# Moving the preparation of the next pair of heads: its uses of the scratch banks spread over six double steps

## The chip, the cores and the metric

The kernel runs on one core of one Trainium2 chip. The metric is device time in microseconds (us) for one execution, the median over runs. The engines that matter here are the tensor engine (PE, whose weight loads have a row of their own, PEld), the vector engine (DVE), the scalar engine (ACT), GpSimd (POOL) and SyncE (SP), whose queue issues nearly all DMAs. Each engine works through its own list of instructions in the order in which the program gives them, and they wait for one another by semaphores.

## The reference, cut to what matters

```python
# q, k, v: (4, 8, 768, 64) float32 ; centroids: (8, 16, 64)
q_assign = argmax(q_n @ c_n.T, -1); k_assign = argmax(k_n @ c_n.T, -1)   # 16 clusters a head
mask   = q_assign[:, :, :, None] == k_assign[:, :, None, :]
scores = where(mask, q @ k.T / sqrt(64), -1e9)
x = (softmax(scores) @ v)                  # -> (3072, 512), heads side by side
h = x @ w_in                               # (512, 2048), float64 in memory
out = (h * clip(h + 3, 0, 6) / 6) @ w_out  # (2048, 512), float64 in memory
```

It is attention in which a query sees only the keys of its own cluster, followed by a feed-forward block (FFN) with a hard-swish gate. Both weight matrices arrive as 64-bit floats and are turned into 32-bit floats on the chip.

## The kernel before, in words

**Tiling.** The 32 heads (4 batches of 8) are worked on as 16 pairs; the two heads of a pair lie side by side on the partitions. A pair takes 12 steps: two halves of 384 queries by six chunks of 128 keys. The main loop (L647) takes two steps at a time, a *double step*, so that a pair has six of them. They are called r0, r2, r4, r6, r8 and r10 here, after the variable `r`, and they are counted by k = 0 to 95 over the kernel: double step k belongs to pair k // 6.

**What a double step holds**, in the order in which it is issued to the engines:

- `scores` twice (L375). On PE: transposed scores of a key chunk against 384 queries for both heads (`ps`, L370), first from the float32 transposes `xf`, then from `xm`, the one-hot cluster codes, which push the scores of a key of another cluster far down. On ACT: `exp` of them into `ex` (L382). On POOL: the running sum `acc` of `ex` (L386, L389).
- `attn_v` twice (L393), for the two steps before: `pv` on PE (L399). At the end of a half, in r0 and r6, ACT copies the sum into `num` (L405).
- In r2 and r8 `divide` (L411) for the half that has ended: PE sums `acc` over the partitions into `pd` (L420), DVE takes the reciprocal `rcp` (L424) and multiplies it with `num` (L425) into `xT`, the input of the FFN. The check `in_range` (two operations of ACT, L432 and L433) is put on a list and issued at the end of the following double step.
- The preparation of the *next* pair, by `prep_items` (L588): four `turn`s (L287), each three transposes on PE into `pqk` (L294) and an ACT copy to `xf` (L296); `cluster_scores` (L303), matmuls into `pcs` (L307) and an ACT copy to `cs`; `route` (L314), three transposes into `pr` (L318) and then on DVE the maximum `mx` (L321) and two comparisons that write `one_hot` (L327), first the part of the queries and then that of the keys; and three `route_turn`s (L343), each four small matmuls into `po` (L350) and an ACT copy to `xm` (L354). `route` also puts `count` (ACT, `seen`, L336, twice) on the list of checks.
- Items of the FFN (`fill`), taken in turns with the items of the preparation: first an item of the FFN, then one of the preparation, and so on. Their matmuls go into `ph`, `py`, `X` and `Y`; ACT and DVE take them out.
- Steps of decoding the weights, a list of 160 (32 chunks of five: `split`, `join`, `power`, `rest`, `total`, L203). All five have an operation on DVE, of about 0.7 us; `split` and `power` have one on ACT too (L214, L230). `split` also issues the DMA of the next chunk. How many are taken in a double step stands in `share` (L613).
- The checks from the list of the double step before.

In r6 the loads of q and k of the pair after next and of v of the next pair are issued on SP (L666).

**Banks.** `scratch` (L167) gives out the PSUM banks for short-lived results: `pqk`, `pcs`, `pr`, `po` and `pd`. Up to k = 47 these are the two banks of the pool `psum_m`, which the FFN's `ph` shares from k = 27 on; from k = 48 it is the single bank of `psum_t`, which up to then serves the decoding (`wtop`). A pair uses scratch eleven times: four `pqk`, one `pcs`, one `pr`, three `po`, two `pd`. A bank can be used again once the engine that empties it is done.

**Stages.** For k = 0 to 26 there is no FFN work. For k = 27 to 47 sixteen items `up` of the FFN's first batch are spread, at most one to a double step. For k = 48 to 51 there are ten FFN items to a double step, from k = 52 one or two, and after k = 95 the rest of the FFN.

The order is written out by hand (`manual_schedule`): each engine has its instructions in the order in which the code issues them.

Of the kernel before, what the change touches and what calls it, by code (L numbers as in the profile page):

```python
# [24 lines left out]
NPAIR = NG // 2  # L25
# [91 lines left out]
def fast_path(ctx, tc, ok, q, k, v, centroids, moe_w_in, moe_w_out, out):  # L117
# [49 lines left out]
    def scratch(shape, name):  # L167

        if st["early"]:
            return psum_m.tile(shape, F32, name=name, tag="m")  # L170
        return psum_t.tile(shape, F32, name=name, tag="t")
# [26 lines left out]
    def load_weights(i):  # L198
        if i < len(chunks):
            st["raw", i] = rawp.tile([P, WC, 2], U32, name="raw")  # L200
            nc.sync.dma_start(st["raw", i], chunks[i][1])
# [85 lines left out]
    def turn(g, part):  # L287
        if part == 0:
            st["xf", g] = xp.tile([P, NC2, P], F32, name="xf")
        qk, xf = st["qk", g], st["xf", g]  # L290
        pt = scratch([P, NHC, P], "pqk")
        for i in range(NHC):
            j = part * NHC + i
            nc.tensor.transpose(out=pt[:, i], in_=qk[:, j // NCH, j % NCH], identity=ident)  # L294
        dst = xf[:, part * NHC : (part + 1) * NHC]
        nc.scalar.copy(out=dst, in_=pt)  # L296
        if part == 3:
            st.pop(("qk", g))
# [4 lines left out]
    def cluster_scores(g):  # L303
        c0, xf = (2 * g) % H * C, st["xf", g]
        ps = scratch([P, 512], "pcs")[:, 0 : NC2 // 4 * P]
        for a in range(4):
            nc.tensor.matmul(  # L307
                ps[a * 2 * C : (a + 1) * 2 * C], lhsT=cnT[:, c0 : c0 + 2 * C], rhs=xf[:, a::4],
                start=True, stop=True,
            )  # L310
        cs = st["cs", g] = rtp.tile([P, NC2 // 4, P], F32, name="cs")
        nc.scalar.copy(out=cs, in_=ps)

    def route(g):  # L314
        cs = st.pop(("cs", g))
        pr = scratch([P, NC2, 2, C], "pr")
        for i in range(NC2 // 4):
            nc.tensor.transpose(out=pr[:, 4 * i : 4 * i + 4], in_=cs[:, i], identity=ident)  # L318
        pr = pr.rearrange("p j t c -> p (j t) c")
        mx = rtp.tile([P, 2 * NC2], F32, name="mx")  # L320
        nc.vector.reduce_max(out=mx, in_=pr, axis=AX.X)  # L321
        oh = one_hot.rearrange("p j (t c) -> p j t c", t=2)[:, :, :, 0:C]
        pr = pr.rearrange("p (j t) c -> p j t c", t=2)
        mx = mx.rearrange("p (j t) -> p j t", t=2)
        halves = [slice(0, NCH), slice(NCH, NC2)]
        for sl, op in zip(halves, (ALU.is_ge, ALU.is_lt)):
            nc.vector.tensor_tensor(  # L327
                out=oh[:, sl], in0=pr[:, sl],
                in1=mx[:, sl].unsqueeze(3).to_broadcast([P, NCH, 2, C]), op=op,
            )  # L330


        def count():
            for a, sl in enumerate(halves):
                seen = rtp.tile([P, NCH, 2, C], BF16, name="seen")
                nc.scalar.activation(  # L336
                    out=seen, in_=oh[:, sl], func=ACT.Copy, scale=1.0 - 2 * a,
                    accum_out=counts[:, a, g : g + 1],
                )

        later.append(count)

    def route_turn(g, part):  # L343
        if part == 0:
            st["xm", g] = xp.tile([P, NC2, P], BF16, name="xm")
        xm = st["xm", g]
        po = scratch([P, 4, P], "po")
        for i in range(4):
            j = part * 4 + i
            nc.tensor.matmul(  # L350
                po[:, i], lhsT=one_hot[:, j], rhs=(ident_q if j < NCH else ident_k),
                start=True, stop=True,
            )
        nc.scalar.copy(out=xm[:, part * 4 : part * 4 + 4], in_=po)  # L354
# [232 lines left out]

    def prep_items(g, r):  # L588

        if g >= NPAIR:  # L590
            return []
        if r in (0, 2):
            return [lambda: turn(g, r), lambda: turn(g, r + 1)]
        return {
            4: [lambda: cluster_scores(g)],
            6: [lambda: route(g)],
            8: [lambda: route_turn(g, 0), lambda: route_turn(g, 1)],
            10: [lambda: route_turn(g, 2)],
        }.get(r, [])

    per_pair = 2 * NCH
    per_batch = NKT * per_pair
    total = NPAIR * per_pair
# [6 lines left out]


    decode = [step for i in range(NW) for step in decoding_steps(i)]
    share = {0: 5, 2: 3, 4: 4, 6: 1, 8: 3, 10: 4}  # L613
    READY, DECODED = per_batch + lag_d, 2 * per_batch

    END = 2 * per_batch + NCH + 2
# [13 lines left out]
    with tc.manual_schedule():  # L630
        nc.scalar.dma_start(cen, centroids.rearrange("h c d -> (h c) d"))
        load(0, "q", "k")
        constants()
        load(0, "v")
        load_weights(0)
        centroid_norm()
        for part in range(4):
            turn(0, part)
        load(1, "q", "k")
        scores_qk(0)  # L640
        scores_qk(1)
        cluster_scores(0)
        route(0)
        for part in range(3):
            route_turn(0, part)

        for n in range(0, total + lag_d + 2, 2):  # L647
            g, r = divmod(n, per_pair)
            for i in (n, n + 1):
                if i < total:  # L650
                    scores(i)
            for i in (n - lag_v, n - lag_v + 1):
                if 0 <= i < total:
                    attn_v(i)
            m = n - lag_d + 1
            if m >= 0 and m % NCH == NCH - 1:
                later.append(divide(m))
            prep = prep_items(g + 1, r)
            if r == 4 and prep:
                prep.pop()()  # L660
            if n == DECODED:
                st["early"] = False
            if m >= 0 and m % per_batch == per_batch - 1:
                fill += (fast_items if m >= per_batch else ffn_items)(m // per_batch)
            if r == 6:
                load(g + 2, "q", "k")  # L666
                load(g + 1, "v")
            want = items_by(n + 2) - done if n < total else len(fill)
            want = min(want, len(fill))
            done += want  # L670
            for i in range(max(len(prep), want)):
                if i < want:
                    fill.pop(0)()
                if i < len(prep):
                    prep[i]()
            for step in decode[: share[r]]:
                step()
            del decode[: share[r]]
            if n >= DECODED and (n - DECODED) // 2 < 8:
                weight_sums((n - DECODED) // 2)  # L680
            for check in checks:
                check()
            checks, later[:] = later[:], []

        for check in checks:
            check()
# [384 lines left out]
```

## Time and profile before

| | |
|---|---|
| median of 3 runs | 1073.45 us (1073.01 to 1074.95) |
| the profiled execution | 1073.12 us, its span 1071.3 us, granted clock of the tensor engine 0.999 |
| PE busy | 1039.3 us (97% of the span), weight loads 670.0 us |
| DVE, ACT, POOL busy | 394.1, 391.2, 294.1 us |
| k = 0 to 26, 27 to 47, 48 to 95 and the rest | about 0 to 133, 133 to 271, 271 to 1071 us |

The profiler's rows give the start of an instruction and its duration. A matmul's end is modelled and covers some of the start of the next, so the time that a matmul really takes up on PE is best read from one start to the next. In an answer of the timeline a row is: start in us, duration in us, engine, line, operation, tiles written and read, form, number of instructions merged, and in brackets the idle time of the engine ahead of it with what ended it.

### The profile page before, as it was taken

Reading aid. Unit: us, or ns where it says so; the run is one execution under the profiler, and the core shown is the slowest. Engines: PE = TensorE matmul, PEld = TensorE weight load, DVE = VectorE, ACT = ScalarE, POOL = GpSimd, SP = SyncE. Lnnn points to the kernel's source line nnn. Section 1 sums busy time; section 2 is a strip of 40 time slices with the busy share of each in tenths; the row PEclk is TensorE's granted clock in tenths of the full one; section 3 lists DMA queues with packets and bytes.
Section 4 is the critical chain, followed back from the end, with each engine's and each line's share of the span. In section 5 each row is a group of like instructions: output and inputs, shape, how many; then the busy total and the mean of one; then the engine's idle time right before and its main releaser. Section 6 shows DMA issues by size and latency. Waiting matters only on the chain.

```text
span 1071.3 us, 12819 instructions
## 1 busy us (share of the span) xinstructions
PE 1039.3 (97%) x5218; PEld 670.0 (63%) x5218; DVE 394.1 (37%) x609; ACT 391.2 (37%) x798; POOL 294.1 (27%) x171
## 2 busy tenths in 40 slices
PE   6999999999999999999999999999999999999997
PEld 3444444444445545676767676667677678888886
DVE  5788865565122103420331331332231232314141
ACT  6888865655212202423332432332423230201010
POOL 3777644444011002223223222323232320000000
PEclk9999999999999999999999999999999999999999
DMA  6444443143001000010202002020100000000000
GB/s 158 100 123 128 129 103 94 59 104 64 10 27 38 1 20 11 22 24 20 45 1 56 10 1 59 6 45 1 35 1 1 20 1 20 1 20 1 20 1 24
DMA packets 83540, 42.89 MB, mean 40 GB/s; under 512 B 76304, under 2 KB 76304, under 8 KB 83472
## 3 DMA queue, kind: packets, MB, share of 16 engines
q1 hardware_dynamic: 83328, 41.95, 15.2%
q8 instruction: 43, 0.70, 0.3%
q14 instruction: 25, 0.20, 0.1%
q10 hardware_dynamic: 144, 0.03, 0.0%
HBM read 35.68 MB, written 6.29 MB: 39 GB/s over the span
## 4 chain that ended last, share of the span: by engine, by line
PE 97%; ACT 2%; DVE 1%; issue 0%; POOL 0%; POOLq 0%; DVEq 0%
PE ph L520 24%; PE ps L370 16%; PE pv L399 13%; PE Y L538 12%; PE X L538 9%; PE ph L456 8%; PE py L473 8%; PE pqk L294 2%; PE pd L420 2%; PE pcs L307 1%; PE po L350 1%; ACT g_sb L443 1%; ACT xm L354 1%; PE pr L318 1%; ACT xf L296 0%
## 5 line engine op out<-in xcount | busy, mean ns | idle before, releaser
L389 POOL TENSOR_TENSOR acc<-acc,ex 128x768 f32<-128x768 f32 x128 | 233.9, 1828 | 398.3 <-ACT ex L382 392.9
L520 PE MATMUL ph<-xT,w_in_sb 128*128 128x256 f32 x1152 | 259.6, 382 | 0.0
L520 PEld LDWEIGHTS ph<-xT,w_in_sb 128*128 128x128 f32 x1152 | 215.4, 190 | 46.0 <-issue 18.1
L382 ACT ACTIVATE ex<-ps 128x768 f32<-128x768 f32 x192 | 148.2, 802 | 121.4 <-PE ps L370 121.1
L443 ACT ACTIVATE g_sb<-ph,half_c 128x512 f32<-128x512 f32 (+1 forms) x104 | 68.0, 654 | 328.1 <-PE ph L520 254.8
L444 DVE SCALAR_TENSOR_TENSOR g_sb<-g_sb,ph 128x512 f32<-128x512 f32 (+1 forms) x104 | 67.2, 646 | 297.3 <-ACT g_sb L443 297.2
L370 PE MATMUL ps<-xf 64*128 64x384 f32 x768 | 165.8, 510 | 0.0
L399 PE MATMUL pv<-ex,vt 128*64 128x384 f32 x768 | 145.1, 499 | 0.0
L424 DVE RECIPROCAL rcp<-pd 128x384 f32<-128x384 f32 x32 | 81.8, 2557 | 84.9 <-PE pd L420 84.6
L386 POOL TENSOR_TENSOR acc<-ex 128x768 f32<-128x768 f32 x32 | 58.0, 1813 | 180.4 <-ACT ex L382 180.4
L399 PEld LDWEIGHTS pv<-ex,vt 128*64 128x64 f32 x768 | 46.6, 136 | 80.0 <-issue 76.2
L370 PEld LDWEIGHTS ps<-xf 64*128 64x128 f32 x768 | 63.5, 187 | 46.0 <-issue 32.2
L456 PE MATMUL ph<-xT,w_in_sb 128*128 128x384 f32 x256 | 87.3, 493 | 0.0
L473 PE MATMUL py<-w_out_sb,g_sb 128*128 128x512 f32 x192 | 84.0, 594 | 0.0
L456 PEld LDWEIGHTS ph<-xT,w_in_sb 128*128 128x128 f32 x256 | 47.2, 190 | 39.4 <-issue 6.0
L538 PE MATMUL Y<-w_out_sb,g_sb 128*128 128x256 f32 x288 | 66.1, 383 | 0.0
L538 PE MATMUL Y<-T,g_sb 128*128 128x256 f32 x288 | 65.3, 380 | 0.0
L538 PE MATMUL X<-w_out_sb,g_sb 128*128 128x256 f32 x288 | 65.3, 380 | 0.0
L473 PEld LDWEIGHTS py<-w_out_sb,g_sb 128*128 128x128 f32 x192 | 35.9, 190 | 44.1 <-issue 43.3
L370 PE MATMUL ps<-xm 64*128 64x384 bf16 x384 | 63.1, 323 | 0.1
L538 PEld LDWEIGHTS Y<-w_out_sb,g_sb 128*128 128x128 f32 x288 | 53.9, 190 | 12.9 <-issue 6.0
L545 DVE TENSOR_TENSOR y<-y,Y 128x256 f32<-128x256 f32 x36 | 15.1, 420 | 127.1 <-PE Y L538 126.5
(88 smaller groups left out, 797.3 us busy)
## 6 DMA issues: line engine op xcount, KB each, us to landing
raw<-in_moe_w_in_dram SPq DMA_DIRECT2D x16, 512.0 KB, 3.6
raw<-in_moe_w_out_dram SPq DMA_DIRECT2D x16, 512.0 KB, 3.5
qk<-in_q_dram SPq DMA_DIRECT2D x32, 192.0 KB, 4.1
qk<-in_k_dram SPq DMA_DIRECT2D x32, 192.0 KB, 4.4
vt<-in_v_dram SPq DMA_DIRECT2D x32, 192.0 KB, 4.3
out_dram<-y SPq DMA_DIRECT2D x24, 256.0 KB, 2.1
cen<-in_centroids_dram ACTq DMA_DIRECT2D x1, 32.0 KB, 1.7
```

The costliest lines, as they stand in the source:

```text
L370: nc.tensor.matmul(st["ps", n][:, t, 0:HALF], lhsT=x[r, NCH + j], rhs=x[r, hf * NHC : (hf + 1) * NHC], start=first, stop=not first,)
L382: nc.scalar.activation(out=ex, in_=sc, func=ACT.Exp, scale=SM_SCALE)
L386: nc.gpsimd.tensor_tensor(out=acc, in0=st["ex", n - 1], in1=ex, op=ALU.add)
L389: nc.gpsimd.tensor_tensor(out=acc, in0=acc, in1=ex, op=ALU.add)
L399: nc.tensor.matmul(pv[t * D : (t + 1) * D], lhsT=vt[:, j, t], rhs=ex[:, t], start=(j == 0), stop=(j == NCH - 1),)
L424: nc.vector.reciprocal(out=rcp, in_=pd)
L443: nc.scalar.activation(out=g, in_=h, func=ACT.Relu, bias=half_c, scale=1.0 / 6.0)
L444: nc.vector.scalar_tensor_tensor(out=g, in0=g, scalar=1.0, in1=h, op0=ALU.min, op1=ALU.mult)
L456: nc.tensor.matmul(hh, lhsT=w_in_sb[:, kt, f * P : (f + 1) * P], rhs=xT[:, kt, hf * HALF : (hf + 1) * HALF], start=(kt == 0), stop=(kt == ...
L473: nc.tensor.matmul(py, lhsT=st["g", f][:, i * P : (i + 1) * P], rhs=w_out_sb[:, f], start=(f == 0), stop=(f == NFT - 1),)
L520: nc.tensor.matmul(ph[:, t * HC : (t + 1) * HC], lhsT=w_in_sb[:, kt, f * P : (f + 1) * P], rhs=xT[:, kt, 2 * m * P : 2 * (m + 1) * P], sta ...
L538: nc.tensor.matmul(bank[:, half * HC : (half + 1) * HC], lhsT=g_sb[:, kind, i], rhs=w[:, i], start=(first and i == 0), stop=(last and i == ...
```

## The change

Eleven uses of scratch stand in the six double steps of a pair as 2, 3, 1, 1, 3, 1 before, counting `divide` in r2 and r8. The change spreads them as 2, 2, 2, 1, 2, 2:

| | before | after |
|---|---|---|
| r0 | turn 0, turn 1 | one-hot group 2 *of the pair itself*, turn 0 |
| r2 | (divide) turn 2, turn 3 | (divide) turn 1 |
| r4 | cluster_scores | turn 2, turn 3 |
| r6 | route | cluster_scores |
| r8 | (divide) one-hot groups 0, 1 | (divide) route |
| r10 | one-hot group 2 | one-hot groups 0, 1 |

One-hot group 2 (`route_turn(g, 2)`, keys 2 to 5 of the pair's six chunks) is thus made in the first double step of the pair that uses it; the first scores that read it are those of r2. `cluster_scores` still comes ahead of the FFN's items of its double step. The steps of decoding per double step change from 5, 3, 4, 1, 3, 4 (20 a pair) to 5, 3, 4, 5, 1, 3 (21 a pair). The loads on SP and `divide` stay where they are.

```diff
     def prep_items(g, r):
 
-        if g >= NPAIR:
-            return []
-        if r in (0, 2):
-            return [lambda: turn(g, r), lambda: turn(g, r + 1)]
-        return {
-            4: [lambda: cluster_scores(g)],
-            6: [lambda: route(g)],
-            8: [lambda: route_turn(g, 0), lambda: route_turn(g, 1)],
-            10: [lambda: route_turn(g, 2)],
-        }.get(r, [])
+        items = []
+        if r == 0 and g > 0:
+            items.append(lambda g=g: route_turn(g, 2))
+        if g + 1 == NPAIR:
+            return items
+        g += 1
+        return items + {
+            0: [lambda: turn(g, 0)],
+            2: [lambda: turn(g, 1)],
+            4: [lambda: turn(g, 2), lambda: turn(g, 3)],
+            6: [lambda: cluster_scores(g)],
+            8: [lambda: route(g)],
+            10: [lambda: route_turn(g, 0), lambda: route_turn(g, 1)],
+        }[r]
...
-    share = {0: 5, 2: 3, 4: 4, 6: 1, 8: 3, 10: 4}
+    share = {0: 5, 2: 3, 4: 4, 6: 5, 8: 1, 10: 3}
...
-            prep = prep_items(g + 1, r)
-            if r == 4 and prep:
+            prep = prep_items(g, r) if n < total else []
+            if r == 6 and prep:
                 prep.pop()()
```

## The prediction

> **What bounds the kernel now.** I read the page first, then the busy time by double step of one pair, then the order of time around the places where PE stands still.
>
> ```profile
> PE 1039.3 (97%) x5218; PEld 670.0 (63%) x5218; DVE 394.1 (37%) x609; ACT 391.2 (37%) x798; POOL 294.1 (27%) x171
> DVE  5788865565122103420331331332231232314141
> ACT  6888865655212202423332432332423230201010
> PEclk9999999999999999999999999999999999999999
> ```
>
> PE is the bound, at a full clock throughout. But ACT and DVE are at 80% in the first slices, where the weights are decoded and the bank users are dense. One pair there (k = 6 to 11):
>
> ```profile
> 40.79:44.83 4.04, 4.04 (x30) 1.96 (x28) 3.90 (x5) 4.01 (x11) 2.44 (x2) 1.00 0.39 119
> 44.83:49.81 4.98, 4.41 (x30) 2.09 (x28) 4.30 (x5) 3.85 (x11) 3.62 (x2) 1.00 0.36 114
> 56.74:62.94 6.20, 5.53 (x40) 2.42 (x38) 3.92 (x5) 4.15 (x13) 4.53 (x3) 1.00 0.91 161
> sum 26.21, PE 24.97 PEld 11.09 DVE 22.32 ACT 22.14 POOL 18.52; mean PE 4.16 PEld 1.85 DVE 3.72 ACT 3.69 POOL 3.09
> ```
>
> Columns: stretch, length, then busy of PE, weight loads, DVE, ACT, POOL. The pair takes 26.2 us, of which ACT is busy 22.1 and DVE 22.3: whatever is moved within it meets two engines with some 4 us to spare. PE idles in the second and third rows (r2, r8), the double steps with three bank users:
>
> ```profile
> 71.66 0.82 PE L420 MATMUL pd<-acc,ones 128*64 128x384 f32 x4
> 72.41 0.55 PE L294 MATMUL pqk<-ident,qk 128*128 128x128 f32 x3
> 72.59 2.56 DVE L424 RECIPROCAL rcp<-pd 128x384 f32<-128x384 f32 x1
> 73.53 0.55 PE L294 MATMUL pqk<-ident,qk 128*128 128x128 f32 x3 [0.57 <-ACT xf L296]
> ```
>
> `pd` keeps one of two banks for the reciprocal's 2.56 us, so turn 3 waits for ACT's copy of turn 2. The two turns take 1.59 (72.41 to 74.00) against 0.81 in r0 (67.70 to 68.51): 0.78 lost. In r8 the two `po` groups take 1.38 (85.68 to 87.06) against 0.55 unhindered (one alone is 0.33, 90.32 to 90.65, and four matmuls more 0.22): 0.83 lost. PE without waits, from start to start: two `scores` 1.82 (87.06 to 88.88), two `pv` 1.44 (88.88 to 90.32; 1.34 ahead of a `pd`), `pd` 0.75, a turn 0.41, `pcs` 0.78 (77.26 to 78.04), `pr` 0.47 (81.30 to 81.77). A pair sums to 24.6; with 1.61 lost it is 26.2, as measured. So 1.61 us a pair is all that spreading can win here.
>
> **What goes.** No matmul is added. For k = 0 to 26 the r8 loss goes from pairs 0 to 3 (4 x 0.83) and the r2 loss from pairs 1 to 4 (4 x 0.78; pair 0 has no divide in r2): -6.4.
>
> **Chain one, new: `route` behind `divide` on DVE, and `po` one double step later.** The rows of its parts:
>
> ```profile
> 85.86 2.56 DVE L424 RECIPROCAL rcp<-pd 128x384 f32<-128x384 f32 x1 [2.17 <-PE pd L420]
> 88.52 0.56 DVE L425 TENSOR_TENSOR xT<-num,rcp 128x384 f32<-128x384 f32 x1
> 81.88 0.56 DVE L321 TENSOR_REDUCE mx<-pr 128x24 f32<-128x384 f32 x1 [0.39 <-PE pr L318]
> 82.47 0.62 DVE L327 TENSOR_TENSOR one_hot<-pr,mx 128x192 bf16<-128x192 f32 x2
> ```
>
> Before, route's DVE work stood alone in r6 with nothing queued ahead. After, it stands behind the reciprocal. From the start of `pd`: reciprocal at 0.93 (84.93 to 85.86), done 3.49; product 3.59 to 4.15; maximum 4.18; one-hot of the queries at 4.77 (0.59 later, 81.88 to 82.47), done 5.12; `po` 0.06 later, 5.18. PE gets there after `pd` 0.75, `pr` 0.47, scores 1.82, `pv` 1.44: 4.48. It stands 0.70, with everything behind it. The product takes up to 0.84 (L425) when POOL adds at the time:
>
> ```profile
> 75.26 0.82 DVE L425 TENSOR_TENSOR xT<-num,rcp 128x384 f32<-128x384 f32 x1
> 71.96 3.70 POOL L389 TENSOR_TENSOR acc<-acc,ex 128x768 f32<-128x768 f32 x2 [1.56 <-ACT ex L382]
> ```
>
> It ended 0.42 after the add (75.66). By my count of ACT's list, the exps of r8 start 0.35 ahead of `pd` in pairs 1 and 2; the two adds then end at 4.2, the product at 4.63, and the wait is 1.18. In pairs 0 and 3 the exps come earlier: 0.70 and 0.80. Sum +3.9, from 2.8 (never met) to 6 (DVE also late, below).
>
> [...]
>
> **Chain two, new: ACT is late for one-hot group 2.** In r10 ACT's list is now two exps, two `xm`, decoding, in_range, count; then r0's exps, `num`, and only then the `xm` that r2's first scores read. The old end of a pair:
>
> ```profile
> 90.75 0.58 ACT L354 CAST xm<-po 128x512 bf16<-128x512 f32 x1
> 91.24 0.72 ACT L230 ACTIVATE wsize<-wsize,w_low 128x512 bf16<-128x512 bf16 x1
> 91.95 0.51 ACT L432 ACTIVATE rcp<-rcp 128x384 f32<-128x384 f32 x1
> 92.59 0.62 ACT L433 ACTIVATE rcp<-rcp,low_c 128x384 f32<-128x384 f32 x1
> 93.20 1.49 ACT L382 ACTIVATE ex<-ps 128x768 f32<-128x768 f32 x2
> ```
>
> From the start of the first `po` in r10: first `xm` at 0.43, two of them to 1.41 (0.49 each); one decoding operation 0.67 (a split's, 87.65 to where the next began); in_range 1.25 (91.95 to 93.20), count 0.83 (88.31 to 89.14): r0's exps at 4.16 and 4.85, `num` 5.54, group 2's `xm` 5.89 to 6.47, PE at 6.53. PE's own way to that matmul: two `po` 0.55, scores 1.82, `pv` 1.44, `po` 0.33, turn 0.41, the float32 part of r2's scores 0.74 (68.51 to 69.25): 5.29. Wait 1.24. At 21 decoding steps a pair, r10 brings a split after pairs 0 and 1 (1.24 each), split and power after pair 2 (1.56 instead of 0.67: 2.13), power after pair 3 (0.72: 1.29). Sum +5.9, from 4 to 7.
>
> Smaller: in pair 0 ACT is the bound (first exps at 16.62) and `pcs`, 0.78, no longer stands where PE would wait for r4's exps: +0.8. R8's scores meet r6's exps, behind in_range, by 0.1 in pairs 1 and 2: +0.2. Up to k = 26: -6.4 + 3.9 + 5.9 + 1.0 = **+4.4**.
>
> **k = 27 to 47.** FFN items (`up`, 2.73 from 140.72 to 143.45) hide both chains where they stand, but `ph` is a third user of two banks. Before, start-to-start excess: r0 0.87 three times, r2 0.83, 0.78, 0.83, r8 1.02, 0.96, 0.83, 1.0: 8.9 with rounding. After, sixteen items on the same k: `ph`, `po`, turn in r0 (0.98 x 3: gate, then `xm`), `ph` and two turns in r4 (0.87 x 2), `ph` and two `po` in r10 (1.02 x 3), group 1's `xm` once 0.24: 8.0. In r2 and r8 `pd` is free 3.49 after its start, PE is there at 3.48: nothing. **-0.9**, from -3 to +1.
>
> **k = 48 on.** One bank. An item of the FFN between two users hides the emptying, except where a double step has a single item: before, k = 52 and 76 (r8, 1.06 each) and 60 and 84 (r0, 0.98 each), 4.1. After, 60 and 84 (1.09, the gate of 0.69 and then `xm`) and 68 (r4, 0.98): 3.2. New: group 1's `xm` is read by the next scores; where a gate of 0.69 stands ahead of it (k = 53, 71, 77) that is 0.35 each, 1.05. **+0.1**, from -1 to +1.
>
> **Queues.** The q and k loads in r6 wait for turn 3, now in r4 instead of r2, and block SP for the weight loads behind them. Before, they were issued at 79.8 with turn 3 done by 74.1; a double step of 4.5 fits, and the loads that follow (issued to 86.2) are read in r0 and r2, two and more double steps on. Costed at nothing; were v late, it would show as waits of `pv` in r2.
>
> **Sum.** +4.4 - 0.9 + 0.1 = +3.6 on the profiled execution's 1073.12, which lies 0.33 below the median: 1077.0.
>
> **Rivals.** *Faster*: neither chain bites, because PE reaches its waits later than I count. Then -6.4 - 0.9 + 0.1: 1066.2. For it speaks ACT idle ahead of r8's `xm` before (1.54) and DVE ahead of `pd` (2.17). It decides if the reciprocal's chain is under 4.48, and the reciprocal alone takes 2.56 of it. *About the same*: one chain only. Without chain two 1071.1, without chain one 1073.1; it decides if ACT's 6.53 falls by 1.2, for instance if in_range (1.25) ran ahead of `xm`; the list says it doesn't. *Slower still*: DVE late. Between `pd` in r2 and in r8 it now has twelve decoding steps in a row, 12 x 0.72 + 3.3 = 11.9 in 12.5 us; L240, median 0.69, took 1.72 beside an add and 2.10 at most. Two such meetings a pair add about 1 us to chain one in four pairs, and later to k = 27 to 47: 1081.5. *That the change does not spread the users*: the built list of PE has them as the table says; none.
>
> **How the numbers follow.** Both chains 0.55, slower still 0.14, one chain 0.22, neither 0.09. Measurement of this kernel can tell about 0.2% (2.1 us) from no change. Of both chains 0.05 stays below that, where each comes out at its lower end; of one chain 0.19 lies within it and 0.03 under 1071.3. So faster 0.12, same 0.24, slower 0.64. The range takes in one chain and a late DVE: 1071.8 to 1081.5; the forecast's own is 1075 to 1079.
>
> **What would show it.** Right: in the pairs up to k = 26, `po` in r10 waits 0.7 to 1.2 for `one_hot`, r2's scores wait 1.2 to 2.1 on ACT, no wait in r2 between `pd` and the turn or in r8, a pair of 26.7 to 27.5 us instead of 26.2. Wrong: a pair under 26, group 2's `xm` ended before the float32 scores of r2, or waits for loads in r0 and r2.

## The result, and the profile after

The changed kernel takes 1084.85 us (median of 4 runs, 1082.79 to 1085.98), the kernel before, run with it on the same chip, 1074.2 (4 runs, 1073.01 to 1075.09). The ratio is 1.0098, 95% interval 1.0078 to 1.0118: slower by about 10 us. The forecast was 1077.0, slower by 3.6. The direction was right, the size was not, and the time lies above the range's end of 1081.5.

The profiled execution took 1082.79 us, 9.67 more than that of before, its span is 1081.0 us. Its page:

```profile
PE 1042.2 (96%) x5218; PEld 668.3 (62%) x5218; DVE 403.0 (37%) x609; ACT 390.1 (36%) x798; POOL 299.3 (28%) x171
DVE  5688976666112203412331321342222231414141
ACT  6788766565302201433323342332333230102010
```

PE issues the same 5218 matmuls. DVE has the same 609 instructions and is busy 9 us longer (403.0 against 394.1): something makes single instructions of DVE longer. Pair 1 by double steps in the view by stretches of time, whose columns are the stretch, its length, then the busy time of PE, weight loads, DVE, ACT and POOL:

```profile
43.44:47.40 3.96, 3.13 (x23) 1.49 (x25) 2.36 (x4) 3.96 (x11) 1.81 (x1) 1.00 0.47 151
47.40:50.68 3.28, 3.28 (x23) 1.53 (x21) 1.49 (x1) 2.63 (x8) 2.23 (x2) 1.00 0.02 8
...
60.50:63.25 2.75, 2.75 (x19) 1.36 (x17) 2.21 (x3) 1.49 (x5) 1.81 (x1) 1.00 1.30 239
63.25:70.62 7.37, 6.25 (x44) 2.37 (x41) 7.09 (x10) 5.21 (x14) 5.97 (x3) 1.00 0.34 117
sum 27.18, PE 25.18 PEld 10.81 DVE 22.52 ACT 21.92 POOL 19.20; mean PE 4.20 PEld 1.80 DVE 3.75 ACT 3.65 POOL 3.20
```

PE no longer stands in r2 (second row) and r8 (third). It stands 1.12 us in r10 (fourth row, 6.25 busy of 7.37) and 0.83 in r0 (first row). So far this is the forecast. But a pair costs more from one to the next. Counted from the first `scores` of r0 to that of the next pair, pairs 1, 2 and 3 take 27.2, 27.6 and 30.4 us (PE starts them at 39.88, 67.06, 94.65 and 125.04); before, 26.2 each. The list of waits from 30 to 133 us, with the waiting instruction, what it waited for, the sum, how many and the longest:

```profile
PE po L350 <- DVE one_hot L327: 7.7, 4, 3.2
...
PE ps L370 <- ACT xm L354: 1.9, 3, 0.6
```

The first row is chain one, in every pair; the second belongs to chain two. The view counts only the time in which PE shows nothing busy, and matmuls' ends are modelled, so the waits are read below from start to start.

**Chain one in pair 0**, DVE's timeline:

```profile
33.57 2.56 DVE L424 RECIPROCAL rcp<-pd 128x384 f32<-128x384 f32 x1 [4.90 <-PE pd L420]
36.23 2.14 DVE L425 TENSOR_TENSOR xT<-num,rcp 128x384 f32<-128x384 f32 x1
38.29 0.55 DVE L321 TENSOR_REDUCE mx<-pr 128x24 f32<-128x384 f32 x1
38.87 0.62 DVE L327 TENSOR_TENSOR one_hot<-pr,mx 128x192 bf16<-128x192 f32 x2
```

and POOL's, ACT's and PE's in the same stretch:

```profile
36.14 1.81 POOL L389 TENSOR_TENSOR acc<-acc,ex 128x768 f32<-128x768 f32 x1
```

```profile
35.10 1.56 ACT L382 ACTIVATE ex<-ps 128x768 f32<-128x768 f32 x2 [1.48 <-PE ps L370]
```

```profile
32.70 0.81 PE L420 MATMUL pd<-acc,ones 128*64 128x384 f32 x4
...
39.28 0.55 PE L350 MATMUL po<-ident_q,one_hot 128*128 128x128 bf16 x6 [2.03 <-DVE one_hot L327]
```

DVE takes the reciprocal in time. The product, 0.56 us by itself, takes 2.14: an add of POOL began 0.09 ahead of it and ended at 37.95, and the product ended 0.42 after that. This add is not one of r8's own two, which are over at 36.06; it is the first of r10, whose `exp` began at 35.10. So `po` starts 6.58 after `pd` instead of PE's own 4.48. In pairs 0 to 3 the start of `po` after `pd` is 6.58, 5.62, 6.03 and 7.72: waits of 2.10, 1.14, 1.55 and 3.24, 8.0 us in all, where 3.9 was forecast.

**Pair 3** has another cause; its product, at 122.61, takes its 0.56. The timeline of all engines there:

```profile
108.18 2.29 DVE L240 SCALAR_TENSOR_TENSOR wunit<-raw,wunit 128x512 f32<-128x512 uint32 x1
...
113.42 2.17 DVE L240 SCALAR_TENSOR_TENSOR wunit<-raw,wunit 128x512 f32<-128x512 uint32 x1
...
119.95 2.55 DVE L424 RECIPROCAL rcp<-pd 128x384 f32<-128x384 f32 x1
...
121.17 0.66 ACT L214 ACTIVATE wsize<-raw 128x512 bf16<-128x512 f32 x1 [3.67 <-DMA raw<-in_moe_w_out_dram]
...
124.08 0.82 PE L350 MATMUL po<-ident_q,one_hot 128*128 128x128 bf16 x6 [3.17 <-DVE one_hot L327]
```

`pd` was issued at 116.36, its reciprocal began 3.59 later instead of 0.93: DVE was behind with its decoding steps, because two of them (L240) took 2.29 and 2.17 instead of 0.68; they started 0.26 and 0.19 behind adds of POOL (at 107.92 and 113.23) and ended 0.54 after them. Which operations of DVE are stretched shows in the durations (least, median, most, in ns) of four of its lines:

```profile
L224 DVE SCALAR_TENSOR_TENSOR wtop<-raw,wtop x32: 682/696/723, 15.7 to 255.5; 128x512 uint32<-128x512 uint32 x32
L245 DVE TENSOR_TENSOR w_in_sb<-wtop,wunit x16: 680/691/693, 17.9 to 119.3; 128x512 f32<-128x512 f32 x16
L240 DVE SCALAR_TENSOR_TENSOR wunit<-raw,wunit x32: 682/693/2295, 17.2 to 257.0; 128x512 f32<-128x512 uint32 x32
L425 DVE TENSOR_TENSOR xT<-num,rcp x32: 557/558/2198, 36.2 to 920.4; 128x384 f32<-128x384 f32 x32
```

Of these four only L240 and L425 are stretched. Both read two tiles in SBUF; `wtop`, an input of the other two, lies in PSUM. Before, L240 was stretched nearly as far, up to 2103 ns, but L425 only to 839.

**Chain two in pair 1**, PE's timeline in r2:

```profile
71.47 0.92 PE L370 MATMUL ps<-xf 64*128 64x384 f32 x4 [0.20 <-ACT ex L382]
73.03 0.34 PE L370 MATMUL ps<-xm 64*128 64x384 bf16 x2 [0.64 <-ACT xm L354]
```

The first `po` of r10 was at 66.46; this matmul follows 6.57 later, forecast 6.53.

**The experiments' measure.** All runs below are compared with the kernel before, run beside them. A profiled pair tells more than the total, and the table under the experiments has pairs 1 to 3 of most. One thing disturbs the total: in some executions the granted clock of PE is 0.50 for 3.4 or 6.8 us within the first 25 us (last section), and kernels that are alike up to `pd` of pair 0 reach it 0.9 to 3.3 us later with such a stretch than without (for instance at 35.56 in e1_share_back and at 32.25 in e5_old_share_product_last). The two profiled executions above, before and after, have none there.

### The profile page after: what moved, and what is told of

It reads as the page before. It is cut to its first block, busy times and chain, and to the rows that moved or that the text cites. A ratio compares the mean times of both kernels' runs of the same rounds, so it can differ in the third digit from the quotient of the medians.

```text
span 1081.0 us, 12825 instructions
## 1 busy us (share of the span) xinstructions
PE 1042.2 (96%) x5218; PEld 668.3 (62%) x5218; DVE 403.0 (37%) x609; ACT 390.1 (36%) x798; POOL 299.3 (28%) x171
## 4 chain that ended last, share of the span: by engine, by line
PE 90%; DVE 4%; ACT 4%; DMA 1%; issue 1%; POOL 0%; DVEq 0%; ACTq 0%; POOLq 0%
PE ph L520 24%; PE ps L370 14%; PE Y L538 12%; PE pv L399 11%; PE X L538 9%; PE ph L456 8%; PE py L473 8%; PE pqk L294 2%; PE pd L420 2%; ACT xm L354 1%; DVE rcp L424 1%; PE pcs L307 1%; ACT g_sb L443 1%; PE po L350 1%; ACT ex L382 1%
## 5 line engine op out<-in xcount | busy, mean ns | idle before, releaser
L389 POOL TENSOR_TENSOR acc<-acc,ex 128x768 f32<-128x768 f32 x128 | 239.1, 1868 | 362.5 <-ACT ex L382 356.7
L386 POOL TENSOR_TENSOR acc<-ex 128x768 f32<-128x768 f32 x32 | 58.0, 1814 | 220.6 <-ACT ex L382 220.6
L424 DVE RECIPROCAL rcp<-pd 128x384 f32<-128x384 f32 x32 | 81.8, 2556 | 93.6 <-PE pd L420 93.6
```

Source lines behind the costliest of these rows:

```text
L386: nc.gpsimd.tensor_tensor(out=acc, in0=st["ex", n - 1], in1=ex, op=ALU.add)
L389: nc.gpsimd.tensor_tensor(out=acc, in0=acc, in1=ex, op=ALU.add)
L424: nc.vector.reciprocal(out=rcp, in_=pd)
```

## Experiments

Two theories stood at the start. One (theory B in the expectations): the new spread of the decoding steps makes DVE late. Two (theory A): the new order puts DVE's product on PE's path, and POOL's adds hold it.

**The spread taken back, and the spread alone.** The first run is the changed kernel with the old spread, the second the kernel before with the new spread.

```diff
 # e1_share_back, in the changed kernel
-    share = {0: 5, 2: 3, 4: 4, 6: 5, 8: 1, 10: 3}
+    share = {0: 5, 2: 3, 4: 4, 6: 1, 8: 3, 10: 4}
 # e2_share_alone, in the kernel before
-    share = {0: 5, 2: 3, 4: 4, 6: 1, 8: 3, 10: 4}
+    share = {0: 5, 2: 3, 4: 4, 6: 5, 8: 1, 10: 3}
```

> The changed kernel with the old decoding steps per double step (5, 3, 4, 1, 3, 4); only the preparation is spread. Theory A (the loss is the wait of po for one_hot behind divide on DVE, made long by POOL's adds and by DVE being late; plus ACT late for one-hot group 2): of the four waits of po in r10 up to k = 23 (8.0 us in the changed kernel) the lateness of DVE in pair 3 (2.7) goes, and ACT's list in r10 gets one power operation in every pair, which takes 1.0 off the second wait: about 1081. Theory B (the new share is what costs): back near 1074 to 1076. Theory C (the spreading alone costs all): 1084 to 1085.

> The kernel before with the new decoding steps per double step (5, 3, 4, 5, 1, 3), the preparation as before. Theory A: po does not stand behind divide here, so no long wait for one_hot; what is left is a split in r8 of pair 3 whose weight chunk comes late behind the q, k and v loads: 1074 to 1077. Theory B (the share costs): 1082 or more.

The first gave 1084.17 us, ratio 1.009 (1.0073 to 1.0106). By the total that is neither the first theory's 1074 to 1076 nor the second's 1081; it lies where the spreading alone would be the cause. But all four executions had a granted clock of only 0.993 to 0.995, and in the profiled one the stretch of half clock at the start is worth the 3.3 us given above; without them the total is about 1081, as the second theory had it. DVE is now in time at every divide (reciprocal 0.93 after `pd`), but the product is held in all four pairs. DVE's and PE's timelines in pair 1:

```profile
64.78 2.56 DVE L424 RECIPROCAL rcp<-pd 128x384 f32<-128x384 f32 x1 [2.08 <-PE pd L420]
67.45 1.98 DVE L425 TENSOR_TENSOR xT<-num,rcp 128x384 f32<-128x384 f32 x1
```

```profile
70.34 0.55 PE L350 MATMUL po<-ident_q,one_hot 128*128 128x128 bf16 x6 [1.94 <-DVE one_hot L327]
```

`po` stands 2.0 in every pair. The second gave 1081.0, ratio 1.0067 (1.005 to 1.0084), where the second theory had 1074 to 1077 for it and the first 1082 or more. So neither part is harmless alone: with the order of before, the new spread makes DVE late, and PE waits for the bank of `pd` at the end of r8, at the worst here:

```profile
149.21 0.38 PE L350 MATMUL po<-ident_q,one_hot 128*128 128x128 bf16 x4 [2.12 <-DVE rcp L424]
```

Both theories thus hold a part, and the two losses do not add: pairs 1 to 3 together take 78.6 us before, 84.2 in the first run, 81.0 in the second, and 85.2 with both.

**Route ahead of the divide**, in r8 for the double steps without FFN work, so that `one_hot` doesn't stand behind the reciprocal and the product.

```diff
 # e3_route_first, in the changed kernel
-            if m >= 0 and m % NCH == NCH - 1:
-                later.append(divide(m))
             prep = prep_items(g, r) if n < total else []
-            if r == 6 and prep:
+            if prep and (r == 6 or r == 8 and n < DECODED):
                 prep.pop()()
+            if m >= 0 and m % NCH == NCH - 1:
+                later.append(divide(m))
```

> The changed kernel with route issued ahead of divide in r8 up to k = 47, so that DVE makes one_hot before the reciprocal; everything else as changed. Theory A: the waits of po for one_hot vanish (8.0 us up to k = 23 and 0.5 in pair 4), the second wait on ACT in r2 (6.2 us) stays: about 1076. If ACT's lateness or the share were the main loss: 1082 or more.

1083.0 us, ratio 1.0097 (1.007 to 1.0125): a miss. The wait for `one_hot` nearly goes (0.3 us left in one pair), and another takes its place, since the late reciprocal now keeps `pd`'s bank from the second `po`:

```profile
121.65 0.27 PE L350 MATMUL po<-ident_q,one_hot 128*128 128x128 bf16 x2 [2.06 <-DVE rcp L424]
```

**The product behind route's DVE work.** The divide's product in r8 is issued after the double step's other items, in front of the decoding steps; with the new spread and with the old.

```diff
 # e4_product_last, in the changed kernel
-        nc.vector.tensor_tensor(
-            out=st["xT", b][:, kt, hf * HALF : (hf + 1) * HALF], in0=num, in1=rcp, op=ALU.mult
-        )
+
+        def product():
+            nc.vector.tensor_tensor(
+                out=st["xT", b][:, kt, hf * HALF : (hf + 1) * HALF], in0=num, in1=rcp, op=ALU.mult
+            )
+
+        if hf == 1:
+            product()
+        else:
+            held.append(product)
...
+            while held:
+                held.pop()()
             for step in decode[: share[r]]:
 # e5_old_share_product_last: the same, and
-    share = {0: 5, 2: 3, 4: 4, 6: 5, 8: 1, 10: 3}
+    share = {0: 5, 2: 3, 4: 4, 6: 1, 8: 3, 10: 4}
```

> The changed kernel with the product of divide in r8 issued behind route's work on DVE; the reciprocal stays ahead of it. Theory A with POOL's adds holding up the product: its 2.14, 1.11 and 1.40 us in pairs 0 to 2 leave the chain to po, which ends about when PE arrives; pair 3, where DVE is late, keeps 2.6: -5 us, about 1080. If the product's stretching did not matter, only 0.6 a pair goes: 1082.5.

> The changed kernel with both: the old decoding steps per double step, and in r8 the product of divide behind route's work on DVE. Theory A (POOL's adds and a late DVE make the wait for one_hot long): with the old share DVE comes to the reciprocal in time, and without the product ahead of it one_hot is ready when PE arrives; the wait of 2.0 us in each of pairs 0 to 3 that stands with the old share goes, and what is left of the loss is the wait on ACT in r2: 1075 to 1077. If it were the spreading itself: 1082 or more.

With the new spread 1080.37, ratio 1.0063 (1.0047 to 1.008), the total as expected, the course only in part: `po` has no wait in pairs 0 and 1, but DVE is late in pair 2 too, not only in pair 3. DVE and PE in pair 2, where `pd` was issued at 85.80:

```profile
88.77 2.55 DVE L424 RECIPROCAL rcp<-pd 128x384 f32<-128x384 f32 x1
```

```profile
92.18 0.55 PE L350 MATMUL po<-ident_q,one_hot 128*128 128x128 bf16 x6 [1.82 <-DVE one_hot L327]
```

With the old spread 1078.1, ratio 1.0048 (1.0028 to 1.0068), a little more than expected. `po` never waits, but now twelve decoding steps, the product and route lie between r8's divide and r2's, and DVE is late there: it is held by adds in two L240, and turn 3 in r4 waits for the bank of r2's `pd`. All engines in pair 2, `pd` being at 72.95:

```profile
70.20 1.87 DVE L240 SCALAR_TENSOR_TENSOR wunit<-raw,wunit 128x512 f32<-128x512 uint32 x1
...
76.35 2.54 DVE L424 RECIPROCAL rcp<-pd 128x384 f32<-128x384 f32 x1
...
78.94 0.31 PEld L294 LDWEIGHTS pqk<-ident,qk 128*128 128x128 f32 x3 [1.21 <-DVE rcp L424]
```

**Without POOL's adds.** The adds of key chunks 2 to 5 are left out, so that the softmax's denominators are the sum over two chunks only; in the changed kernel and, as a control, in the kernel before.

```diff
 # e6_after_no_adds, e7_before_no_adds
         elif j > 1:
             acc = st["acc", g, hf]
-            nc.gpsimd.tensor_tensor(out=acc, in0=acc, in1=ex, op=ALU.add)
```

> The changed kernel without POOL's adds of key chunks 2 to 5 (L389), so that the sums under the division hold two chunks of six alone; POOL is nearly idle. Theory A (an operation of DVE with two operands in SBUF stands until POOL's add is over): the operations L240 and L425 take their least, 0.68 and 0.56, DVE is in time, the wait of po for one_hot falls to 0.7 a pair: 1079 to 1080. If POOL does not matter: 1084 to 1085.

> The control: the kernel before without POOL's adds of key chunks 2 to 5 (L389), the sums under the division again of two chunks alone. Theory A: DVE loses its 8 us of waiting for POOL here too, but nothing on the path of PE waits for it: 1073 to 1074.5.

The changed kernel falls to 1077.38, ratio 1.004 (1.0024 to 1.0055); the kernel before stays: 1074.03, ratio 0.9996 (0.9986 to 1.0005). By the medians the adds cost the new order 7.5 us, between the two profiled executions, neither of which has half clock at the start, 5.8; the old order they cost nothing. What is left is 3.2 us by the medians and 3.9 between the profiles; with a product that is never held (four times 0.70 for chain one) the forecast would have been +2.5. Without adds the product (L424 there) takes at most 559 ns (L240 still up to 2287; L386, the first addition of a half, stays), and `po` starts 5.00 to 5.07 after `pd`, so that it waits 0.52 to 0.59 in each pair, where the forecast, without a stretched product, had 0.70. The list of waits now has:

```profile
PE po L350 <- DVE one_hot L327: 2.0, 4, 0.5
```

**The count later.** With the old spread and the product behind, ACT's counting is moved out of the list that r2's `xm` stands behind.

```diff
 # e8_count_late, on e5_old_share_product_last
-        later.append(count)
+        counting.append(count)
...
             checks, later[:] = later[:], []
+            if r == 2:
+                while counting:
+                    counting.pop()()
```

> The changed kernel with the old share, the product behind route, and count issued at the end of r2 instead of r10. Theory A: ACT's list between po in r10 and group 2's copy is shorter by 0.83, so the wait in r2 falls from about 1.3 to 0.5 in four pairs: 3 us less than the same kernel with count in r10, 1072 to 1074. If the wait on ACT in r2 were not what is left: no difference between the two.

1079.31, ratio 1.0048 (1.0032 to 1.0064), a miss: the three executions with a granted clock of 0.998 lie at 1077.4 to 1078.3, where e5_old_share_product_last has its own three (1077.2 to 1078.1). The wait for `xm` shrinks by 0.83 a pair, as said, and PE then waits longer for the late reciprocal in r4 (1.9 instead of 1.1 in pair 1, from turn 2 to turn 3 less the 0.41 of a turn). On this spread DVE is the bound there, and what PE gains elsewhere is given back.

**Both cures at once, with balanced spreads.** Twenty decoding steps a pair, as in the kernel before, ten on each side of the divides (5, 3, 4, 3, 1, 4), or nine between r8's and r2's and eleven between r2's and r8's (4, 4, 4, 3, 1, 4).

```diff
 # e9_three_one, on e4_product_last
-    share = {0: 5, 2: 3, 4: 4, 6: 5, 8: 1, 10: 3}
+    share = {0: 5, 2: 3, 4: 4, 6: 3, 8: 1, 10: 4}
 # e10_four_pairs: the same with
+    share = {0: 4, 2: 4, 4: 4, 6: 3, 8: 1, 10: 4}
```

> The changed kernel with the product behind route's DVE work, and with the twenty decoding steps of a pair spread 5, 3, 4, 3, 1, 4: ten between the two divides on each side. If DVE's lateness at the divides is a matter of where its work lies, both divides find it in time, both waits (po in r10, turn 3 in r4) go, and only the wait behind ACT's list in r2 is left, which is about what the removed waits gave: 1074 to 1076. If DVE is full whatever the spread (its work and its waits for POOL's adds), the lateness shows at one of the divides again: 1078 or more.

> The same with 4, 4, 4, 3, 1, 4: nine steps between r8's divide and r2's, eleven between r2's and r8's. If the place of the work decides, this differs from 5, 3, 4, 3, 1, 4 by one step (0.7 to 2.3 us of DVE's time) moved from before turn 3 to before po: within 1.5 us of it, and the lateness, where there is any, at r8's divide and not at r2's. If DVE is full whatever the spread: 1078 or more.

1073.62 and 1073.26, ratios 0.9995 (0.9985 to 1.0004) and 0.9993 (0.9983 to 1.0003). The whole loss is gone. In both, each of the four pairs is the same: reciprocal 0.86 to 0.93 after `pd`, `po` at 4.48, PE's own time. Pair 1 of the second on DVE and PE (the product is L427 in this kernel):

```profile
59.67 2.56 DVE L424 RECIPROCAL rcp<-pd 128x384 f32<-128x384 f32 x1 [0.54 <-PE pd L420]
62.14 0.49 DVE L321 TENSOR_REDUCE mx<-pr 128x24 f32<-128x384 f32 x1
62.67 0.62 DVE L327 TENSOR_TENSOR one_hot<-pr,mx 128x192 bf16<-128x192 f32 x2
63.21 1.11 DVE L427 TENSOR_TENSOR xT<-num,rcp 128x384 f32<-128x384 f32 x1
```

```profile
63.22 0.51 PE L350 MATMUL po<-ident_q,one_hot 128*128 128x128 bf16 x6
```

The product is still held (1.11), but behind `one_hot`, where PE doesn't wait for it. So DVE was not full whatever the spread; the loss lay in where its work stood.

**The loads of q, k and v behind the decoding steps of r6**, to price the late weight chunk of pair 3.

```diff
 # e11_loads_behind, in the changed kernel
-            if r == 6:
-                load(g + 2, "q", "k")
-                load(g + 1, "v")
...
             del decode[: share[r]]
+            if r == 6:
+                load(g + 2, "q", "k")
+                load(g + 1, "v")
```

> The changed kernel with the loads of q, k and v issued at the end of r6 instead of before its decoding steps. Pair 3's weight chunk is then ahead of them in SP's queue, and ACT's 3.67 us wait for it in r8 goes. If that wait set the end of po's wait in pair 3 or the start of the scores behind it, the kernel gains 1 to 3 us (1081.5 to 1084); if DVE's lateness in pair 3 covers it, nothing (1084 to 1086).

1086.25, ratio 1.0114 (1.0097 to 1.0131): no gain. In pair 3 SP's wait for the chunk's buffer, PE and DVE show:

```profile
SPq L201 <- DVE wunit L240: 28.7, 4, 12.3
```

```profile
129.16 0.82 PE L350 MATMUL po<-ident_q,one_hot 128*128 128x128 bf16 x6 [5.06 <-DVE one_hot L327]
```

```profile
121.75 2.23 DVE L240 SCALAR_TENSOR_TENSOR wunit<-raw,wunit 128x512 f32<-128x512 uint32 x1
...
124.62 2.55 DVE L424 RECIPROCAL rcp<-pd 128x384 f32<-128x384 f32 x1
```

There are two buffers for raw chunks, and SP's load waits for the L240 that reads the older one: that L240 ended at 118.79 and the load was issued at 118.87, so it can't come earlier than DVE lets it. ACT's wait for the chunk fell from 3.67 only to 2.26, where it was expected to go. With the loads moved, a third L240 stood behind an add (2.23) and the reciprocal began 5.07 after `pd`. The queue is not the cause of pair 3's loss; DVE is.

**Without the adds, and with the product behind**: the changed kernel with the edits of e6_after_no_adds and e4_product_last (again without the adds of key chunks 2 to 5).

> The changed kernel without POOL's adds of key chunks 2 to 5 (denominators of two chunks only, so this part of the computation is left out) and with the product behind route's DVE work. If the terms add up, the wait of po that was left without the adds (0.78 to 0.85 us a pair, four pairs) goes: 1077.4 less 3.2, 1074 to 1074.5, so what stays of the change is chain two against the removed waits, about nothing. If moving the product only moves the lateness even with DVE free of POOL, 1076.5 to 1078.

1075.32, ratio 1.0019 (1.0009 to 1.0029), between the two expected ranges. The wait of `po` goes, as said: pairs 1 and 2 take 26.04 instead of 26.62. These 0.58 a pair are what the wait was worth; four of them are 2.3, and the totals differ by 2.1. The expectation had put the wait at 0.78 to 0.85. Pair 3 takes 26.78, because ACT has a decoding operation more ahead of `xm`, issued in pair 2's r10, as the forecast's chain two has it for the 21 steps of this spread (2.13 instead of 1.24). ACT's L214 waits 2.24 for pair 3's late weight chunk here too, and PE stands nowhere behind it. So chain two comes out as forecast with chain one out of the way: from `po` to the matmul on `xm` 6.56, 6.56, 7.40 and 6.60, forecast 6.53, 6.53, 7.42 and 6.58.

**The count later, with the balanced spreads**: the edit of e8_count_late on each.

> 5, 3, 4, 3, 1, 4 and the product behind route's DVE work, with route's counting on ACT put at the end of r2, out of the list that r2's copy of xm waits behind. The wait of r2's scores for xm (1.2 to 1.3 us a pair in the run without this) shrinks by the 0.83 us that the same step gave with the old spread. If DVE now has room at both divides: four pairs of 0.8 us, 1070 to 1071.5, faster than both kernels. If a faster PE makes DVE late again at one of the divides: 1072.5 to 1075.

> The same with 4, 4, 4, 3, 1, 4, which has one decoding step less between r8's divide and r2's, where DVE was late before with the counting late. If DVE has room: 1069.5 to 1071. If it is late again: 1072.5 to 1075.

With 5, 3, 4, 3, 1, 4: 1069.47 us (1069.27 to 1070.48), ratio 0.9954 (0.994 to 0.9967), a little under the expected 1070 to 1071.5. It beats both kernels. The pair takes 25.15 us, 0.83 less than without the late count, and DVE stays in time. The profiled spans, both without half clock at the start, differ by 3.5 us (1067.8 against 1071.3), the medians by 4.95. PE in pair 1, r2:

```profile
67.15 0.92 PE L370 MATMUL ps<-xf 64*128 64x384 f32 x4
68.18 0.34 PE L370 MATMUL ps<-xm 64*128 64x384 bf16 x2
```

From the first `po` (62.41) to the matmul on `xm` it is 5.77 now, against 6.57 after the change and PE's own 5.29. With 4, 4, 4, 3, 1, 4: 1074.09, ratio 1.0001 (0.9992 to 1.001), no gain: in pairs 1 to 3 the reciprocal of r8 begins 2.44 after `pd` instead of 0.93, and PE waits. PE, then DVE in pair 1:

```profile
64.72 0.55 PE L350 MATMUL po<-ident_q,one_hot 128*128 128x128 bf16 x6 [1.30 <-DVE one_hot L327]
```

```profile
53.60 2.06 DVE L240 SCALAR_TENSOR_TENSOR wunit<-raw,wunit 128x512 f32<-128x512 uint32 x1
...
58.60 2.06 DVE L240 SCALAR_TENSOR_TENSOR wunit<-raw,wunit 128x512 f32<-128x512 uint32 x1
```

The same two L240 took 1.31 and 0.69 without the late count. The counting at the end of r2 puts ACT's exps of r4, and with them POOL's adds, 0.8 us later after r2's `pd` (4.05 instead of 3.22): the adds began at 53.29 and 58.30, each 0.3 ahead of an L240, and held it.

**The spread alone, and the control.** The changed kernel with 4, 4, 4, 3, 1, 4 and the product in its place, and the kernel before with the same spread.

```diff
 # e15_four_pairs_alone, in the changed kernel
-    share = {0: 5, 2: 3, 4: 4, 6: 5, 8: 1, 10: 3}
+    share = {0: 4, 2: 4, 4: 4, 6: 3, 8: 1, 10: 4}
 # e16_before_four_pairs, in the kernel before
-    share = {0: 5, 2: 3, 4: 4, 6: 1, 8: 3, 10: 4}
+    share = {0: 4, 2: 4, 4: 4, 6: 3, 8: 1, 10: 4}
```

> The changed kernel with the spread 4, 4, 4, 3, 1, 4 alone: the product stays ahead of route's DVE work. DVE comes to the divide in time, but the product can stand behind POOL's add, as with the old spread (1.98 to 2.05 us, po's wait 2.0 us a pair): 1073.3 plus four times 2.0, 1080 to 1082. If the spread is the cure and the product's hold is only a matter of where POOL's add falls: 1075.5 to 1077 (po's wait 0.8 us a pair, as forecast).

> Control: the kernel before with the spread 4, 4, 4, 3, 1, 4. If the spread acts only by bringing DVE in time to what the change put on PE's path, the kernel before, in which DVE's lateness cost nothing, stays within 1 us of its time: 1073 to 1075. If the spread is better of itself: below 1072.5.

1082.45, ratio 1.0071 (1.0056 to 1.0087). DVE is in time, but the product is held in each pair, and `po` waits 2.0:

```profile
67.43 1.98 DVE L425 TENSOR_TENSOR xT<-num,rcp 128x384 f32<-128x384 f32 x1
```

The control gave 1075.25, ratio 1.0013 (1.0003 to 1.0022), a little above what was expected. Its pairs take 26.2 as in the kernel before; its profile has 1.2 us more at the start, at half clock, and 1.8 more at k = 27 to 47. The spread is no gain of itself.

The time of pairs 1, 2 and 3 in us, from the first `scores` to the next pair's, by the two cures:

| decoding steps in r0 to r10 | product ahead of route's DVE work | product behind it |
|---|---|---|
| 5, 3, 4, 1, 3, 4 (old) | 28.3, 28.0, 28.0 | 27.2, 27.2, 27.2 |
| 5, 3, 4, 5, 1, 3 (the change) | **27.2, 27.6, 30.4** | 26.0, 28.1, 29.6 |
| 4, 4, 4, 3, 1, 4 | 28.3, 28.0, 28.0 | 26.0, 26.0, 26.0 |
| 5, 3, 4, 3, 1, 4 | | 26.0, 26.0, 26.0 |
| the same, count late | | 25.15, 25.15, 25.15 |

The kernel before has 26.2 in each. Both cures are needed: against the 26.0 with both, the spread alone leaves 2.0 us a pair, the product alone 1.2 in each pair or up to 3.6 in one. In the first and third rows' 28.3, in the second row's 29.6 and at the end of its 30.4 a stretch of half clock falls; in the first and third it is worth the 0.3 by which pair 1 is longer than pairs 2 and 3.

## Why the prediction was wrong in size

- **What goes, -6.4: right.** The waits between two users in r2 and r8 are gone in the profile after.
- **Chain one: the step that failed.** The forecast put 3.9 on it, by pairs 0.70, 1.18, 1.18 and 0.80; it measured 8.0, by pairs 2.10, 1.14, 1.55 and 3.24. The mechanism was right (without the adds, its wait is 0.52 to 0.59 where the forecast without a stretched product had 0.70), the term was mis-sized. Pair 1 came as forecast; the 4.1 that were missing lie in the others:
  - Pair 0 has 1.4. The forecast looked at the adds of r8 alone and rightly found them over there, but the first add of r10 begins just ahead of the product and holds it. So it is in pair 1 of e1_share_back too, where r10's `exp` begins at 66.25, its add at 67.20 and the product at 67.45, for 1.98.
  - Pair 2 has 0.4, because an L240 (88.47, its 0.69) stretched the add ahead of the one that held the product, to 2.22 (88.61).
  - Pair 3 has 2.4, and there the product was not held at all: DVE came late, as the point after this one says.

  The price that the forecast used, "the product takes up to 0.84 (L425) when POOL adds at the time", was taken from rows that had met only the tail of an add, in the row of 0.82 its last 0.40 us (75.26 to 75.66). With an add of 1.81 begun 0.09 ahead of it the product took 2.14 (pair 0 here), and with one begun 0.24 or 0.25 ahead 1.98 (e15_four_pairs_alone and e1_share_back, pair 1). The end is the same in all: in the row of 0.82, in pairs 0 to 2 here and in those two the product ended 0.41 to 0.42 after the add.
- **"Slower still: DVE late", priced at 1 us a pair: the mechanism is there, the price was not.** Up to k = 26 it came in pair 3 alone, and was 2.66 (the reciprocal 3.59 after `pd` instead of 0.93). The count of 11.9 us of work in 12.5 left no room: two L240 at 2.29 and 2.17 are 3.1 over the least.
- **Chain two, +5.9: right.** From the first `po` to the matmul on `xm` it measured 6.56, 6.57, 7.40 and 6.81, forecast 6.53, 6.53, 7.42 and 6.58; the waits sum to 6.2.
- **The queues, costed at nothing: right in cost, not in course.** The loads block SP as described, and pair 3's chunk came 3.67 late for ACT. But it cost nothing: moving the loads gained nothing, and in the run without adds and with the product behind the chunk comes 2.24 late and PE doesn't wait.
- **Not in the forecast: the clock.** After PE had stood 3.2 us in pair 3, the granted clock was 0.50 for 3.4 us, and two `scores` took 2.82 instead of 1.82. Nearly all of that fell into the wait for `xm` that chain two had there anyway: from `po` to the matmul on `xm` it is 6.81, against 6.60 at the same place in e12_no_adds_product_last, at full clock. So the clock cost the kernel about 0.2.
- **Up to k = 26** the loss, with the work that is moved across that line (`pcs`, 0.78) put back, is 8.9 against 4.4. Chain one has 4.1 of the difference and chain two 0.3, the clock's 0.2 among them; the small terms, put at 1.0, come out at 1.1 as what is left.
- **k = 27 to 47: -0.9 forecast, +0.7 measured**, within the term's range. In the balanced kernels that stretch takes 138.13 us against 138.81 after the change and 137.65 before, so DVE's lateness has about 0.7 of it (at k = 28, `pr` waits 0.55 for a reciprocal); the gain of 0.9 that was forecast doesn't come even with DVE in time, and why was not followed further.
- **k = 48 on: +0.1 forecast, about +0.1 measured.** The three stretches are counted from the first `scores` of k = 27 and of k = 48 on PE, which before are at 130.46 and 268.11 us.
- **The rivals.** "One chain only, without chain one" was put at 1073.1; the kernels in which chain one is cured take 1073.26 and 1073.62. That this fits so well is partly chance: in them chain two is about 0.7 smaller, as they take twenty decoding steps a pair, and the 0.9 of k = 27 to 47 doesn't come. The count moved later is worth the 0.83 a pair that ACT's list gives it in the kernel at 1069.47; with two other spreads (e8_count_late, e14_four_pairs_count_late) a late DVE took it back.

## What to carry to other kernels

An operation that gives an off-path engine's result can be late for free until a reordering puts somebody behind it; when work is moved behind a queue, price each operation ahead of it by its worst row beside the neighbour that holds it, not by its median, and ask whether the row met that neighbour whole or only at its end. Count the neighbour's work of the following step too: here it was the add of r10, not those of r8, that held the product. When such a chain bites, look for what can be moved behind the awaited result (here the product, 0.56 us of work, 2 us on the path), and place the rest of that engine's work so that each deadline has about the same work ahead of it; one cure alone may only move the wait. A change that removes bank waits but fills the queue of the engine that empties the banks must be counted on both.

## What the runs showed of the hardware

- **In the meetings below, of an add of POOL with the product or an L240, the one that began second was stretched, at leads from 0.02 us on.** In the changed kernel the add began 0.09 ahead of the product in pair 0 and the product took 2.14; later there an add at 212.83 was 0.02 ahead of a product, which took 2.20. In the kernel with 4, 4, 4, 3, 1, 4 and the product behind, an L240 began at 57.71, 0.07 ahead of an add; it took its 0.69 and the add was stretched:

```profile
57.78 2.30 POOL L389 TENSOR_TENSOR acc<-acc,ex 128x768 f32<-128x768 f32 x1 [0.41 <-ACT ex L382]
```

  An add that began first took 1.81 (at 36.14 in the changed kernel). Moving ACT's count, an operation of 0.8 us on a third engine, was enough to turn 0.69 and 1.31 into 2.06 twice.
- **PE's granted clock was 0.50 after a wait of 3.17 us in the changed kernel and after one of 1.82 with the product behind.** The 3.41 us ahead of such a stretch and the first 3.41 of it, in the first (pair 3) and in e4_product_last (pair 2), with the granted clock behind POOL's busy time:

```profile
120.29:123.70 3.41, 0.62 (x4) 0.00 (x0) 3.27 (x4) 2.15 (x4) 1.64 (x2) 1.00 0.49 159
123.70:127.11 3.41, 3.03 (x16) 2.05 (x18) 3.31 (x6) 2.35 (x7) 2.95 (x2) 0.50 0.00 0
```

```profile
90.34:93.75 3.41, 1.53 (x16) 0.77 (x15) 3.34 (x7) 1.14 (x3) 3.25 (x3) 1.00 0.46 154
93.76:97.17 3.41, 3.41 (x14) 1.36 (x16) 3.24 (x6) 3.31 (x12) 0.77 (x1) 0.50 0.00 0
```

  The stretches at the start of e14_four_pairs_count_late and e16_before_four_pairs last about 3.4 us too, those at the start of e9_three_one and e15_four_pairs_alone 6.8. There, where PE is busy for 0.7 to 1.2 of the 2 us from 14 to 16, they come in some executions and not in others: the profiles of before and after have none. Ahead of the two stretches above PE was busy for 0.62 and 1.53 us of 3.41. Which waits bring it on is not settled: in e1_share_back a wait of 1.94 to 1.95 stands in each of four pairs, and only the first is followed by half clock (the pair behind it takes 28.3 us, the two next 28.0). Nor is its price what PE's rows say: in the changed kernel, where two `scores` took 2.82 instead of 1.82, it was about 0.2 us on the path, because PE would have waited for ACT in any case.
